# The landmarks' sums kept once: two products with the identity in place of a copy and a transpose

## The chip, the cores and the metric

The kernel runs on one core of one Trainium2 chip. A core has TensorE (PE, with its weight loads shown apart as PEld), VectorE (DVE), ScalarE (ACT), GpSimd (POOL) and SyncE (SP, which issues most of the transfers here). The metric is the device time of one execution in microseconds; the kernel before took 1337.75 us in the median of 3 runs (1334.39 to 1339.83).

## The reference

The program computes a Nystrom attention with 32 landmarks for 8 batches of 8 heads, 576 positions and 64 values per head, then a layer with a squared ReLU (512 to 2048 to 512), then a layer of 8 experts of which each token takes one. All is in float32. The change touches the landmarks alone: each is the mean of 18 neighbouring positions of q or of k, and every score of the attention has a landmark on one side.

```python
def _attn_ref(q, k, v):
    m = 32
    q_lm = q.reshape(B, H, m, S // m, D).mean(axis=3)
    k_lm = k.reshape(B, H, m, S // m, D).mean(axis=3)
    A = sm(q, k_lm)
    Bm = sm(q_lm, k_lm)
    C = sm(q_lm, k)
    Z = Bm.transpose(0, 1, 3, 2) / (norm1(Bm) * norminf(Bm) + 1e-06)
    for _ in range(6):
        Z = 2 * Z - Z @ Bm @ Z
    return A @ Z @ C @ v

def _moe_ref(x, w_in, w_out):
    r = np.maximum(x @ w_in, 0.0)
    return (r * r) @ w_out

# then, for each expert e and its tokens:
#   out[mask] = gate * eom * (np.maximum(x[mask] @ w1[e], 0) @ w2[e])
```

## The kernel before

One batch after the other passes through two kinds of work. The attention of a batch is a chain of small steps (`unit`), and the first layer of a batch is a stream of large matmuls (`gemm`). The attention of batch 0 stands alone at the start (`prologue`), beside the conversion of the weights `w_in` and `w_out` (`convert`, lines 146 to 167: ACT, DVE and POOL work on each piece). From then on the steps of later batches are woven between the matmuls of `gemm`: at each point of `gemm` a counter decides whether the next step of the attention is issued (`point`). The last stage are the experts (`experts`), with no attention in it.

In `gemm`, `hp` (line 998) is the hidden layer in six matmuls of 288 columns, ACT makes its ReLU (1009) and square `gh` (1014), DVE the rest `gl` of the square (1011, 1015), and `second` adds 12 matmuls into `acc` (1048). Nearly all matmuls of these streams are in fp32r with 128 x 128 weights.

A landmark step begins with the sums. q and k of a batch come in two groups of four heads (`hg`), 128 partitions (4 heads x 32 landmarks) by 18 positions by 64 values. `sums` adds the 18 positions on DVE in two halves of 32 values (line 382) and lets POOL copy the 64 sums beside themselves (line 385), so that a row has them twice. `landmarks` transposes these 128 columns on PE (line 349, with `self.ident`): the 64 values of a landmark then lie on partitions 0 to 63 and again on 64 to 127, four heads by 32 landmarks along the free axis. ACT copies both groups from the bank in PSUM to `lm` (line 447). The scores need both halves, since one half of the heads (or of the positions) is taken from partitions 0 to 63 and the other from 64 to 127. There are 8 batches x q and k x 2 groups = 32 sums, copies and transposes.

Names in the rows: `t` is a group of q or k as loaded, `sums` the sums, `bank` a bank of PSUM, `ident` the identity, `lm` the landmarks, `x` q or k with values on partitions, `eu`, `dg` and `bc` the iteration for the inverse, `wt` the small matrix Z C v of a batch, which is multiplied with `w` (a piece of `w_in`) in two matmuls into the two halves of a bank (line 872 loads `w`), `gb` and `ab` the split operands of `hp`. Attention matmuls are issued through `matmul` (line 346) and `transpose` (line 349), so rows are told apart by their tiles.

The order on each engine isn't the order of the code: the framework's scheduler deals the instructions out by priorities and its own reckoning of when each is ready. The attention of batch 0 has high priority (`URGENT`), and `follow` holds a few instructions behind others. On one engine the instructions run in the order dealt, so one that waits holds all behind it.

Of the kernel before, what the change touches and what calls it, by code (L numbers as in the profile page):

```python
# [9 lines left out]
F32 = mybir.dt.float32  # L10
# [4 lines left out]
ALU = mybir.AluOpType  # L15
AX = mybir.AxisListType
# [3 lines left out]
B, H, S, D = 8, 8, 576, 64  # L20
# [63 lines left out]
class Kernel:  # L84
# [290 lines left out]
    def sums(self, u, nm, hg):  # L375

        if hg == 0:
            u[nm + "s"] = self.sm.tile([128, 2, 2, D], F32, tag=f"{nm}s", name="sums", bufs=1)
        s, t = u[nm + "s"][:, hg], self.qk[nm, u["b"], hg]
        for d in range(0, D, D // 2):  # L380
            ds = slice(d, d + D // 2)
            self.nc.vector.tensor_reduce(  # L382
                out=s[:, 0, ds], in_=t[:, :, ds].rearrange("p s d -> p d s"), axis=AX.X, op=ALU.add
            )
        self.nc.gpsimd.tensor_copy(out=s[:, 1], in_=s[:, 0])

    def transposed(self, u, nm, hg, i):

# [50 lines left out]
    def landmarks(self, u, nm):  # L439
        nc = self.nc  # L440
        pd = self.bank()
        for hg in range(2):
            self.transpose(
                pd[:, 128 * hg:128 * hg + 128], u[nm + "s"][:, hg].rearrange("p c d -> p (c d)"), self.ident
            )
        lm = u[nm + "l"] = self.sm.tile([128, 2, 4, LM], F32, tag=f"{nm}l", name="lm", bufs=1)
        nc.scalar.copy(out=lm.rearrange("p g h l -> p (g h l)"), in_=pd[:, 0:256])

# [1049 lines left out]
```

## Time and profile before

| | |
|---|---|
| median of 3 runs | 1337.75 us (1334.39 to 1339.83) |
| profiled execution | 1340.34 us, span 1338.5 us |
| mean granted clock of TensorE | 0.977 |
| PE busy | 1275.7 us, 95% of the span |
| DVE busy | 781.5 us, 58% |
| ACT busy | 633.6 us, 47% |
| POOL busy | 384.5 us, 29% |
| sums on DVE (line 382) | 64 x 1165 ns, 71.2 us |

Busy time is the time in which an engine had an instruction at work; PE's matmuls are pipelined, so that starts follow each other more closely than their durations say. The shares are means over stages that are bound by different things, so the rows below are taken by stretch. In the chain of waits a piece such as "PE bank L349 x2" is what PE did from one start to the next piece's.

### The profile page before, as it was taken

The page shows a single profiled execution, that of the slowest core. Times are in us where ns is not written, and L with a number is a line of the kernel's source. Part 1 is how long each engine was busy: PE and PEld are TensorE (multiplying, and loading weights), DVE is VectorE, ACT ScalarE, POOL GpSimd, SP SyncE. Part 2 cuts the span into 40 slices and gives each one's busy share as a digit, 9 for nine tenths or more (in the row PEclk, how much of TensorE's full clock was granted, in tenths as well). Part 3 has the DMA queues.
Part 4 walks back from the last instruction along what each step waited for, and adds up shares of the span by engine and source line. Part 5 has one row for each costly group of instructions (what it writes and reads, how often), then busy time and mean ns, then how long its engine had stood idle before and what let it go on. Part 6 is the DMA issues. An engine that isn't in the chain of part 4 may idle for free.

```text
span 1338.5 us, 25101 instructions
## 1 busy us (share of the span) xinstructions
PE 1275.7 (95%) x9458; PEld 1114.2 (83%) x9458; DVE 781.5 (58%) x1743; ACT 633.6 (47%) x1402; POOL 384.5 (29%) x311
## 2 busy tenths in 40 slices
PE   6587999999999999999999999999999999999997
PEld 4276868688788888898989999998888888888886
DVE  7999868768769897687653433454423233233231
ACT  5596454445535557545654344344334334334331
POOL 3566112113013034313622112024323323233120
PEclk7588999999999999999999999999999999999999
DMA  9866283462623247613652112014344354342321
GB/s 324 273 222 192 86 269 85 173 199 89 217 70 112 72 127 211 172 63 95 206 146 67 43 35 67 1 48 146 99 130 139 100 156 120 109 150 92 116 93 38
DMA packets 126587, 172.38 MB, mean 129 GB/s; under 512 B 10558, under 2 KB 84062, under 8 KB 126462
## 3 DMA queue, kind: packets, MB, share of 16 engines
q1 hardware_dynamic: 126030, 170.11, 41.6%
q8 instruction: 76, 1.25, 0.4%
q0 software_dynamic: 288, 0.43, 0.1%
q14 instruction: 49, 0.40, 0.1%
q10 hardware_dynamic: 144, 0.20, 0.0%
HBM read 128.19 MB, written 42.51 MB: 128 GB/s over the span
## 4 chain that ended last, share of the span: by engine, by line
PE 74%; DVE 11%; DMA 7%; ACT 3%; issue 2%; POOL 1%; SPq 1%; POOLq 0%; DVEq 0%; ACTq 0%
PE acc L1048 24%; PE hp L1238 15%; PE y L1274 13%; PE hp L998 11%; PE bank L346 6%; PE y L1286 2%; DMA raw<-in_moe_w_in_dram 2%; DVE sums L382 2%; DVE gl L1015 2%; DMA g<-gs 2%; DVE g L1011 1%; PE pl L1075 1%; DVE m L164 1%; DMA w<-win 1%; DMA t<-in_q_dram 1%
## 5 line engine op out<-in xcount | busy, mean ns | idle before, releaser
L1048 PE MATMUL acc<-gh,wo 128*128 128x288 f32 x2048 | 459.2, 300 | 1.6 <-POOL wo L191 0.7
L1048 PEld LDWEIGHTS acc<-gh,wo 128*128 128x128 f32 x2048 | 344.1, 190 | 27.1 <-issue 18.2
L1048 PE MATMUL acc<-gl,wo 128*128 128x288 f32 x1024 | 290.3, 301 | 10.2 <-DVE gl L1015 9.7
L998 PE MATMUL hp<-ab,gb 128*128 128x288 f32 x1536 | 254.8, 301 | 0.9 <-ACT r L1009 0.5
L998 PEld LDWEIGHTS hp<-ab,gb 128*128 128x128 f32 x1536 | 217.7, 189 | 19.6 <-issue 6.9
L1011 DVE TENSOR_TENSOR g<-r 128x288 f32<-128x288 f32 x239 | 130.3, 546 | 162.5 <-ACT r L1009 161.7
L1009 ACT ACTIVATE r<-hp 128x288 f32<-128x288 f32 x256 | 105.8, 413 | 245.1 <-PE hp L998 240.6
L1238 PEld LDWEIGHTS hp<-xs,s 128*128 128x128 f32 x1536 | 210.7, 188 | 9.0 <-issue 0.9
L1238 PE MATMUL hp<-xs,s 128*128 128x288 f32 x1536 | 215.5, 295 | 0.0
L1048 PEld LDWEIGHTS acc<-gl,wo 128*128 128x128 f32 x1024 | 194.6, 190 | 22.8 <-DVE gl L1015 17.5
L1274 PE MATMUL y<-s,h 128*128 128x512 f32 x768 | 190.3, 395 | 0.0
L1274 PEld LDWEIGHTS y<-s,h 128*128 128x128 f32 x768 | 141.0, 188 | 29.4
L1015 DVE TENSOR_TENSOR gl<-g,gh 128x288 fp32r<-128x288 f32 x256 | 143.2, 560 | 26.8 <-ACT gh L1014 8.9
L191 POOL TENSOR_TENSOR s<-r,s 128x512 fp32r<-128x512 f32 x64 | 83.1, 1299 | 245.6 <-ACT s L188 245.6
L191 DVE TENSOR_TENSOR s<-r,s 128x512 fp32r<-128x512 f32 x64 | 53.1, 830 | 154.4 <-ACT s L188 154.4
L191 POOL TENSOR_TENSOR gb<-gr,gb 128x512 fp32r<-128x512 f32 x56 | 74.5, 1331 | 226.6 <-ACT gb L188 143.6
L188 ACT CAST s<-r 128x512 fp32r<-128x512 f32 x128 | 78.2, 616 | 118.8 <-PE y L1286 92.6
L1247 DVE SCALAR_TENSOR_TENSOR h<-hp,h 128x64 fp32r<-128x64 f32 (+2 forms) x192 | 62.6, 354 | 109.5 <-ACT h L1244 109.5
L1014 ACT ACTIVATE gh<-r 128x288 fp32r<-128x288 f32 x256 | 114.4, 447 | 6.4
L1244 ACT ACTIVATE h<-hp 128x288 fp32r<-128x288 f32 x128 | 52.6, 411 | 132.1 <-PE hp L1238 118.2
L382 DVE TENSOR_REDUCE sums<-t 128x32 f32<-128x576 f32 x64 | 71.2, 1165 | 9.3 <-DMA t<-in_q_dram 5.8
L191 POOL TENSOR_TENSOR xs<-xr,xs 128x1152 fp32r<-128x1152 f32 x16 | 45.7, 2860 | 68.3 <-ACT xs L188 63.2
(195 smaller groups left out, 1350.8 us busy)
## 6 DMA issues: line engine op xcount, KB each, us to landing
r<-in_moe_w_dram SPq DMA_DIRECT2D x128, 256.0 KB
w<-win SPq DMA_DIRECT2D x80, 256.0 KB
gr<-g SPq DMA_DIRECT2D x56, 256.0 KB
t<-in_k_dram SPq DMA_DIRECT2D x16, 576.0 KB
t<-in_q_dram SPq DMA_DIRECT2D x16, 576.0 KB
v<-in_v_dram SPq DMA_DIRECT2D x48, 192.0 KB
x_d<-x SPq DMA_DIRECT2D x16, 576.0 KB
xr<-x_d SPq DMA_DIRECT2D x16, 576.0 KB
```

The source lines that it names most:

```text
L188: hi = self.nc.scalar.copy(out=t[:, 0], in_=raw)
L191: (lo_eng or self.nc.gpsimd).tensor_tensor(out=t[:, 1], in0=raw, in1=t[:, 0].bitcast(F32), op=ALU.subtract)
L346: self.last_pe = self.nc.tensor.matmul(out, **kw)
L382: self.nc.vector.tensor_reduce(out=s[:, 0, ds], in_=t[:, :, ds].rearrange("p s d -> p d s"), axis=AX.X, op=ALU.add)
L998: mm = nc.tensor.matmul(hp[:, 0:HC], lhsT=g[:, l, hg, fs], rhs=at[:, r, hg, :], start=(i == 0), stop=(i == 5))
L1009: nc.scalar.activation(out=r, in_=hp[:, 0:HC], func=ACTF.Relu, scale=1.0 / 256)
L1011: nc.vector.tensor_tensor(out=g2, in0=r, in1=r, op=ALU.mult)
L1014: nc.scalar.activation(out=gh, in_=r, func=ACTF.Square)
L1015: nc.vector.tensor_tensor(out=gl, in0=g2, in1=gh.bitcast(F32), op=ALU.subtract)
L1048: nc.tensor.matmul(acc[m][:, 0:HC], lhsT=self.wo[f][:, l, ms], rhs=r, start=(f == 0 and i == 0), stop=(f == NFC - 1 and i == 2),)
L1238: nc.tensor.matmul(hp[:, 0:HC], lhsT=s1[:, l, kk, :], rhs=xs[j, c][:, r, kk, :], start=(k == 0), stop=(k == 3 * KD - 1),)
L1274: mm = nc.tensor.matmul(acc[t], lhsT=l, rhs=s2[:, r, :], start=(first and k == 0), stop=(last and k == 2))
```

## The change

`sums` keeps the 64 sums once (the tile has half the size), and the copy on POOL is gone. `landmarks` no longer transposes. For each group it makes two matmuls with the sums as weights (128 x 64) and the identity as moving operand (128 columns), one into partitions 0 to 63 and one into 64 to 127 of the same columns of the bank. That is four matmuls in f32 per landmark step in place of two transposes, 64 in all in place of 32; the profile shows such an f32 matmul as two rows. DVE's reductions and ACT's copy to `lm` are as they were.

```diff
     def sums(self, u, nm, hg):
         if hg == 0:
-            u[nm + "s"] = self.sm.tile([128, 2, 2, D], F32, tag=f"{nm}s", name="sums", bufs=1)
+            u[nm + "s"] = self.sm.tile([128, 2, D], F32, tag=f"{nm}s", name="sums", bufs=1)
         s, t = u[nm + "s"][:, hg], self.qk[nm, u["b"], hg]
         for d in range(0, D, D // 2):
             ds = slice(d, d + D // 2)
             self.nc.vector.tensor_reduce(
-                out=s[:, 0, ds], in_=t[:, :, ds].rearrange("p s d -> p d s"), axis=AX.X, op=ALU.add
+                out=s[:, ds], in_=t[:, :, ds].rearrange("p s d -> p d s"), axis=AX.X, op=ALU.add
             )
-        self.nc.gpsimd.tensor_copy(out=s[:, 1], in_=s[:, 0])
...
     def landmarks(self, u, nm):
         pd = self.bank()
         for hg in range(2):
-            self.transpose(
-                pd[:, 128 * hg:128 * hg + 128], u[nm + "s"][:, hg].rearrange("p c d -> p (c d)"), self.ident
-            )
+            for p in (slice(0, D), slice(D, 2 * D)):
+                self.matmul(
+                    pd[p, 128 * hg:128 * hg + 128], lhsT=u[nm + "s"][:, hg], rhs=self.ident, start=True, stop=True
+                )
```

The scheduler deals the changed program out anew. Lines behind `landmarks` are one higher in the new program (1048 is 1049, 998 is 999). On PE, the start of the program, batch 0 before (rows of one instruction or of several alike, with their number in the list):

```order
1 L349 MATMUL bank<-ident,t 128x128 x18
2 L349 MATMUL bank<-ident,sums 128x128 x4
3 L346 MATMUL bank<-x,lm 32x288 x7
4 L346 MATMUL bank<-lm 32x32 x8
5 L346 MATMUL bank<-x,lm 32x288 x9
```

and now:

```order
1 L349 MATMUL bank<-ident,t 128x128 x16
2 L346 MATMUL bank<-ident,sums 64x128
3 L349 MATMUL bank<-ident,t 128x128
4 L346 MATMUL bank<-ident,sums 64x128
5 L349 MATMUL bank<-ident,t 128x128
6 L346 MATMUL bank<-ident,sums 64x128 x6
7 L346 MATMUL bank<-x,lm 32x288 x7
8 L346 MATMUL bank<-lm 32x32 x8
9 L346 MATMUL bank<-x,lm 32x288 x9
```

The products of the first groups stand between the transposes of `t`, and the eight of batch 0 are issued one by one as their sums come.

On PE in batch 2, the landmarks of k between the matmuls of `gemm`, before:

```order
304 L1048 MATMUL acc<-gl,wo 128x288
305 L1048 MATMUL acc<-gh,wo 128x288
306 L349 MATMUL bank<-ident,sums 128x128 x2
307 L1048 MATMUL acc<-gl,wo 128x288
308 L1048 MATMUL acc<-gh,wo 128x288
309 L1048 MATMUL acc<-gl,wo 128x288
310 L1048 MATMUL acc<-gh,wo 128x288
311 L998 MATMUL hp<-ab,gb 128x288 x6
312 L1048 MATMUL acc<-gh,wo 128x288
```

and now:

```order
300 L1049 MATMUL acc<-gh,wo 128x288
301 L346 MATMUL bank<-ident,sums 64x128 x4
302 L1049 MATMUL acc<-gl,wo 128x288
303 L1049 MATMUL acc<-gh,wo 128x288
304 L1049 MATMUL acc<-gl,wo 128x288
305 L1049 MATMUL acc<-gh,wo 128x288
306 L999 MATMUL hp<-ab,gb 128x288 x6
307 L346 MATMUL bank<-w,wt_1890 64x512
308 L1049 MATMUL acc<-gh,wo 128x288
```

Four matmuls stand where two transposes stood, and around them the matmuls of `wt` with `w` have moved against those of `gemm`.

On POOL, the first rows behind the constants, before:

```order
11 L385 COPY sums<-sums 128x64 x4
12 L167 TENSOR_TENSOR wf<-m,r 128x512 x7
13 L385 COPY sums<-sums 128x64
14 L167 TENSOR_TENSOR wf<-m,r 128x512
15 L477 TENSOR_TENSOR aa<-aa,ma 128x576
16 L167 TENSOR_TENSOR wf<-m,r 128x512 x2
17 L477 TENSOR_TENSOR aa<-aa,ma 128x576
```

and now:

```order
11 L167 TENSOR_TENSOR wf<-m,r 128x512 x8
12 L478 TENSOR_TENSOR aa<-aa,ma 128x576
13 L167 TENSOR_TENSOR wf<-m,r 128x512 x2
14 L478 TENSOR_TENSOR aa<-aa,ma 128x576
15 L167 TENSOR_TENSOR wf<-m,r 128x512 x2
16 L191 TENSOR_TENSOR ab<-at,ab 128x576
```

The copies of the sums are gone and nothing else has moved here; the conversion's additions (`wf`) follow each other directly.

## Rows read from the trace of the kernel before

**Rows 1.** stretches: us, busy us of PE PEld DVE ACT POOL, clock, DMA

```profile
0.00:80.00 80.00, 51.82 (x445) 30.34 (x446) 70.56 (x152) 50.63 (x115) 35.58 (x39) 0.74 0.92 298
80.00:130.00 50.00, 40.13 (x367) 35.58 (x366) 48.28 (x76) 39.10 (x93) 34.84 (x26) 0.86 0.59 181
130.00:700.00 570.00, 555.74 (x4655) 478.15 (x4656) 434.42 (x985) 302.41 (x701) 156.18 (x140) 1.00 0.47 142
```

**Rows 2.** the chain of waits from 130 to 700 us, its shares by line

```profile
by line: PE acc L1048 32.3%; PE hp L998 15.7%; PE bank L346 13.2%; DMA g<-gs 3.6%; issue 3.5%; DVE sums L382 3.4%; DVE gl L1015 2.8%; DVE g L1011 2.5%; DMA w<-win 2.0%; DVE x L413 1.6%; DMA v<-in_v_dram 1.5%; PE bank L349 1.5%; PE pl L1075 
```

**Rows 3.** the tile of the sums: ns min/median/max, starts

```profile
L382 DVE TENSOR_REDUCE sums<-t x64: 1111/1169/1225, 4.7 to 595.7; 128x32 f32<-128x576 f32 x64
L385 POOL COPY sums<-sums x32: 230/266/563, 7.0 to 596.9; 128x64 f32<-128x64 f32 x32
...
L349 PE MATMUL bank<-ident,sums x32: 270/272/477, 8.7 to 597.9; 128*128 128x128 f32 x32
...
  PE bank L349: 5.2, 5
```

**Rows 4.** waits of PE, 130 to 700 us: us, times, longest

```profile
PE acc L1048 <- DVE gl L1015: 4.4, 7, 1.1
...
PE bank L349 <- POOL sums L385: 1.4, 2, 0.9
```

**Rows 5.** timeline at 420 us around one transpose: start, us

```profile
420.42 0.24 POOL L385 COPY sums<-sums 128x64 f32<-128x64 f32 x1 [3.38 <-DVE sums L382]
...
420.71 0.44 PE L349 MATMUL bank<-ident,sums 128*128 128x128 f32 x2 [0.43 <-POOL sums L385]
```

**Rows 6.** timeline to 15 us, the last copy and transpose of batch 0

```profile
13.23 0.36 POOL L385 COPY sums<-sums 128x64 f32<-128x64 f32 x1 [1.86 <-DVE sums L382]
...
13.65 0.48 PE L349 MATMUL bank<-ident,sums 128*128 128x128 f32 x1 [1.89 <-POOL sums L385]
```

**Rows 7.** chain of waits, 162 to 169 us: start, us, what

```profile
162.07 1.87 PE bank L346 x8
163.94 0.99 PE hp L998 x6
...
165.46 1.01 PE bank L346 x4
166.47 0.73 PE acc L1048 x4
167.20 0.22 PE bank L349 x2
167.42 0.54 PE acc L1048 x4
167.96 0.80 PE hp L998 x6
```

**Rows 8.** the lines of f32 matmuls on line 346, by operands and shape

```profile
L346 PE MATMUL bank<-x,lm x512: 402/427/686, 14.6 to 638.2; 64*32 64x288 f32 x171
...
L346 PE MATMUL bank<-eu,dg x168: 217/275/350, 130.1 to 649.2; 128*128 128x96 f32 x140, 128*128 128x64 f32 x28
...
L346 PE MATMUL bank<-w,wt x96: 592/592/644, 162.0 to 361.7; 128*64 128x512 f32 x96
```

**Rows 9.** the chain of waits from 148 to 154 us

```profile
151.93 0.42 PE bank L346 x4
152.34 0.82 PE hp L998 x6
```

**Rows 10.** timeline, DVE's subtractions beside POOL's work

```profile
415.58 1.45 POOL L191 TENSOR_TENSOR gb<-gr,gb 128x512 fp32r<-128x512 f32 x1 [0.91 <-ACT gb L188]
...
415.81 1.54 DVE L1015 TENSOR_TENSOR gl<-g,gh 128x288 fp32r<-128x288 f32 x1
...
427.34 0.44 DVE L1015 TENSOR_TENSOR gl<-g,gh 128x288 fp32r<-128x288 f32 x1
427.48 0.40 POOL L385 COPY sums<-sums 128x64 f32<-128x64 f32 x1 [3.35 <-DVE sums L382]
```

## The prediction

> **What bounds the kernel now.** I read the busy time of the engines by stretch first, then the chain of waits, then everything that touches the tile of the sums, and last the PE timeline beside matmuls of the new shape.
>
> The stretches [rows 1] show three regimes. Up to 80 us DVE works 70.56 of 80 us and the DMA share is 0.92, while PE works 51.82 us. From 80 to 130 us DVE works 48.28 of 50 us, so it is the bound, and PE has 10 us to spare. From 130 to 700 us PE works 555.74 of 570 us, so only 14.3 us are free. The last transpose of sums starts at 597.9 us [rows 3], so nothing that the change touches lies behind 700 us. The chain of the third stretch [rows 2] says the same less sharply: its three largest entries are PE's lines, 61% together, and DVE's sums have 3.4%. So in the third stretch a microsecond added to PE costs close to a microsecond, and one taken from POOL, 156.18 us busy of 570, is worth nothing unless PE or DVE waited for it.
>
> The sums [rows 3]: 64 reductions on DVE, 32 copies on POOL of 266 ns, 32 transposes on PE. PE stood idle before a transpose, waiting for a copy, 5.2 us in five waits [rows 3]. Only two of these, 1.4 us, are in the third stretch [rows 4], where 24 of the 32 transposes lie (those of batches 2 to 7); the other three belong to batch 0, 13.65 us being the last.
>
> **The change part by part.** *The copies go.* 32 copies of 0.27 us are 8.6 us of POOL's 384.51. POOL isn't the bound in any stretch, and PE's two late waits don't vanish whole. At 420.42 us the copy itself starts only when DVE's reduction has ended, and PE starts 0.29 us later [rows 5]. The hop of 0.29 us goes, the reduction stays, and DVE's sums are what is late next. Two waits: 0.6 us. What stood behind the copies on POOL, the subtractions for gb and aa, may start earlier; with POOL busy 156.18 of 570 us [rows 1] I price that at nothing.
>
> *In the prologue* the last copy starts at 13.23 us and PE at 13.65 [rows 6], so 0.42 us are saved. Against the median of 0.272 [rows 3] this transpose took 0.48 us, in a stretch whose mean granted clock is 0.74 [rows 1], so partly at the lower level (1.2 GHz); four rows of products in its place take longer by what I estimate below from wt, 0.215 us a pair at 2.4 GHz and twice that at 1.2, and so give back most of the 0.42. The order on DVE, which does 70.56 of these 80 us, is unchanged up to batch 1. I take zero, and half a microsecond either way for the range.
>
> *The transposes become products.* Each landmark had two transposes. The chain shows such a pair as one piece of 0.22 us, followed by four acc matmuls in 0.54 us [rows 7], 0.135 each, their usual pace. Now it has four f32 products with 64 columns of weights and 128 moving columns, two for the lower and two for the upper half of the partitions. No row of before has just this. The nearest is wt, 128 x 64 weights into the two halves of a bank, in f32 too, with 512 moving columns. One pair takes 1.01 us and two pairs together take 1.87 [rows 7]: a second pair adds 0.86, so a train has about 0.15 us of its own and 0.86 per pair at 512 columns, or 0.215 at 128 if it goes with the columns. (That it does go with the columns is borne out by the medians of a row in [rows 8], 592 at 512, 427 at 288, 275 at 96.) What stands behind such a train is late too: acc x4 takes 0.73 us instead of 0.54, hp x6 0.99 instead of 0.80 [rows 7], so 0.20 us each time.
>
> The Trainium skill, "TensorEngine Tiling (Array Packing)", Key Properties, says that changing the tiling mode drains TensorE; by that rule the 0.20 us is the drain, and the trace agrees that there is one. The same page's Restrictions say that column tiling excludes transpose mode for f32, so the halves could not be had as two cheap transposes; no run here shows that.
>
> A landmark's train is then 0.15 + 2 x 0.215 = 0.58, with the 0.20 behind it 0.78, against 0.22 before. In the new order batches 2 to 7 have 24 pairs in 14 trains, two of which stand beside a wt train of the same shape, so that 12 pay the fixed 0.35 us: 24 x 0.215 + 12 x 0.35 - 24 x 0.11 = 5.2 + 4.2 - 2.6 = 6.7 us. The bounds come from the rows on both sides. Low: a train of two f32 matmuls at 96 columns without halves takes 0.42 with hardly a late start behind it (hp 0.82) [rows 9], so +0.2 per landmark, 2.4 us for 12. High: 288 columns in place of 128, 0.15 + 2 x 0.48 + 0.20 - 0.22 = 1.1 per landmark, 13 us. I take 6.7, since 128 lies near 96.
>
> Batch 1 has its eight products in one train between 80 and 130 us: 4 x 0.215 + 0.35 - 0.44 = 0.8 us, covered by PE's 10 us of slack beside DVE. If that cover were gone, 0.8 us would be added.
>
> *What hides the 6.7 us* is only PE's own idle time of 14.3 us. Where PE would have waited anyway, a train costs nothing. I leave 85% standing: 5.7 us. Less the two hops this is +5.1 us.
>
> *The order.* The program's instructions are dealt out anew by a scheduler, and from batch 2 on acc, hp and attention steps stand in other places on PE, DVE, ACT and SP. The work is the same. I price the deal at 0 in the sum and keep it as a rival.
>
> **The sum.** The profiled execution took 1340.34 us with a span of 1338.5; +5.1 gives 1345.4. Its median in three runs is 1337.75, 2.6 lower, so the same change gives 1342.9; I say 1342.5. That is +0.36%. About 0.5% (6.7 us) is what a measurement of this kernel can tell from no change, so this counts as no change, not far from the edge of slower at 1344.4.
>
> **The rivals.** *A, the order loses (slower).* In the third stretch PE waits for DVE's gl in seven places with 4.4 us [rows 4]. If in the new order the reductions of 1.17 us stand more often ahead of gl on DVE, and PE's idle 14.3 us grow by half, 7 us are added: 1350. It decides as soon as 2 us more are lost than I reckoned. For it: DVE is busy in 76% of the stretch, 434.42 of 570 us [rows 1], so PE has little lead on it. Against it: before has the same mixture, and the deal can win as well.
>
> *B, the halves don't overlap (slower).* Then a pair takes 0.43 us, 24 x 0.215 = 5.2 us more: 1348. Against it speaks wt, two of whose pairs in 1.87 us would take about twice that if they ran one behind the other.
>
> *C, PE's idle time swallows the price (same).* 14.3 us would be room for 6.7. Then only the hops remain: 1337. Against it: the trains stand between acc and hp, where PE works through, and only two of the 24 late transposes had PE waiting for a copy.
>
> *D, DVE is relieved (faster).* On DVE an elementwise operation with two SBUF inputs suffers beside POOL: gl took 1.54 us beside POOL's subtraction at 415.81, but 0.44 beside the copy at 427.48 [rows 10]. If each copy had held DVE for its own time, 8.6 us would come back, all of it where DVE bounds or feeds PE. With the five waits of 5.2 us gone whole and the low price of 2.4 us this gives 1337.75 - 8.6 - 5.2 + 2.4 = 1326. Against it is the row at 427.48: there the copy was the longer one, 0.40 instead of 0.24, and gl was not. The Trainium skill, "GPSIMD Engine Reference", Specifications, says that GpSimd shares its SBUF interfaces with VectorE, with contention for DVE instructions with two SBUF inputs; by that rule alone D would be likely, and the trace agrees for POOL's subtraction, not for its copy.
>
> **How the numbers follow.** Forecast 0.50 (own range 1338 to 1347; three tenths of it beyond 1344.4), A 0.18, B 0.06, C 0.12, D 0.14. Slower: 0.15 + 0.18 + 0.06 = 0.39. Same: 0.35 + 0.12 = 0.47. Faster: 0.14. The range reaches down past C into the upper part of D, since a deal that wins also ends there, and up past A: 1331 to 1352.
>
> **What would show it.** On PE the sums' group has 64-column weights and mean rows near 0.3 us; a landmark's piece in the chain is near 0.58 us instead of 0.22, and hp or acc behind it are 0.20 longer. POOL has 32 instructions fewer and PE no wait for POOL's sums. PE's idle time from 130 to 700 us stays near 14 us while the stretch grows by about 5. It is wrong if the stretch after 130 us is shorter than before (D or a lucky deal), if a piece lasts 0.9 us or more (B), if the idle time falls by as much as the products add (C), or if PE's waits for gl grow by several microseconds (A). A change before 130 us of more than 1 us would also be outside this account.

## The result and the profile after

The changed kernel took 1345.23 us (median of 6 runs, 1342.84 to 1347.08) beside 1337.83 us (1334.39 to 1339.83) of the kernel before: ratio 1.0052, 95% interval 1.0036 to 1.0068, so 7.0 us slower, between 4.8 and 9.1. A second series of runs gave 1.0055 [1.0036, 1.0074]. The forecast was 1342.5, the range 1331 to 1352. The number lies inside; what follows shows that half of the reasons behind it did not hold.

The stretches of the changed kernel, in the columns of [rows 1]:

```profile
0.00:80.00 80.00, 52.32 (x456) 30.88 (x457) 71.13 (x152) 50.87 (x115) 33.63 (x32) 0.72 0.91 299
80.00:130.00 50.00, 37.92 (x383) 31.70 (x382) 48.11 (x79) 38.49 (x91) 34.05 (x25) 0.94 0.61 193
130.00:700.00 570.00, 558.37 (x4678) 476.59 (x4678) 434.54 (x978) 300.31 (x697) 148.37 (x117) 1.00 0.46 141
```

From 130 to 700 us PE works 558.37 us where it worked 555.74, so its idle time is 11.6 us instead of 14.3, and the work that used to end in this stretch now ends about 6 us later. DVE is as busy as it was, POOL 7.8 us less.

The tile of the sums in the changed kernel, which answers to [rows 3] (ns min/median/max, starts; below, PE's waits that an instruction on this tile ended: us, times):

```profile
L346 PE MATMUL bank<-ident,sums x128: 272/273/476, 8.3 to 600.0; 128*64 128x128 f32 x128
L382 DVE TENSOR_REDUCE sums<-t x64: 1107/1171/1220, 4.7 to 598.6; 128x32 f32<-128x576 f32 x64
...
  PE bank L346: 3.5, 5
```

64 products leave 128 rows. POOL's copies are gone. A reduction on DVE takes 1171 ns at the median, where it took 1169.

PE's waits from 130 to 700 us in the changed kernel, which answer to [rows 4]:

```profile
PE acc L1049 <- DVE gl L1016: 5.9, 12, 1.1
...
PE bank L346 <- DVE sums L382: 0.8, 3, 0.4
```

POOL is no longer waited for. DVE's gl is waited for in 12 places, against 7.

A piece of the chain of waits of the changed kernel around one landmark, the same place as [rows 7] (start, us, what):

```profile
165.59 1.01 PE bank L346 x4
166.60 0.73 PE acc L1049 x4
167.32 0.59 PE bank L346 x8
167.91 0.72 PE acc L1049 x4
```

The train of four products is the piece of eight rows with 0.59 us, where two transposes took 0.22. The four acc matmuls behind it take 0.72 instead of 0.54.

Last, two rows of ACT's timeline in the kernel before: activations that take a half batch out of `acc`, as milestones (start, us):

```profile
141.12 0.69 ACT L1054 ACTIVATE x<-acc 128x288 f32<-128x288 f32 x2
...
319.98 0.41 ACT L1054 ACTIVATE x<-acc 128x288 f32<-128x288 f32 x1 [0.32 <-PE acc L1048]
```

The same two in the changed kernel:

```profile
146.39 0.70 ACT L1055 ACTIVATE x<-acc 128x288 f32<-128x288 f32 x2
...
319.83 0.41 ACT L1055 ACTIVATE x<-acc 128x288 f32<-128x288 f32 x1 [0.31 <-PE acc L1049]
```

At 141 us the changed kernel is 5.3 us behind, at 320 us it is level again. A price that adds up landmark by landmark does not look like that, although one milestone of one trace is a weak sign. So two theories went to the chip. *Price*: the products themselves cost the time. *Order*: the new deal of instructions on the engines costs it.

### The profile page after: what moved, and what is told of

The parts are those of the page before. It is cut to its first block, busy times and chain, and to the rows that moved or that the text cites. A ratio compares the mean times of both kernels' runs of the same rounds, so it can differ in the third digit from the quotient of the medians.

```text
span 1344.7 us, 25243 instructions
## 1 busy us (share of the span) xinstructions
PE 1282.9 (95%) x9554; PEld 1115.8 (83%) x9554; DVE 783.1 (58%) x1743; ACT 633.4 (47%) x1402; POOL 374.0 (28%) x279
## 4 chain that ended last, share of the span: by engine, by line
PE 76%; DVE 10%; DMA 5%; ACT 3%; issue 3%; POOL 1%; SPq 0%; POOLq 0%; DVEq 0%; ACTq 0%
PE acc L1049 25%; PE hp L1239 15%; PE y L1275 13%; PE hp L999 12%; PE bank L346 7%; PE y L1287 2%; DVE sums L382 2%; DMA g<-gs 2%; PE pl L1076 1%; DVE m L164 1%; DVE gl L1016 1%; DVE g L1012 1%; DVE m L163 1%; DMA gr<-g 1%; DMA t<-in_q_dram 1%
## 5 line engine op out<-in xcount | busy, mean ns | idle before, releaser
L382 DVE TENSOR_REDUCE sums<-t 128x32 f32<-128x576 f32 x64 | 71.2, 1166 | 11.1 <-DMA t<-in_q_dram 8.5
```

What stands on the lines that cost most here:

```text
L382: self.nc.vector.tensor_reduce(out=s[:, ds], in_=t[:, :, ds].rearrange("p s d -> p d s"), axis=AX.X, op=ALU.add)
```

## The experiments

Both kernels leave their order to the scheduler. To part work from order, most of the kernels below carry a recorder. It lists each engine's instructions as the program issues them and, at the end, holds them to a table with dependencies that need no semaphore:

```diff
+        for e, t in _ORDER.items():
...
+            for k in order:
...
+                for i in made[k]:
+                    if last is not None:
+                        self.follow(i, last)
+                    last = i
```

The table is the order of the kernel before, or of the changed one, or one spliced from both. In the traces of these kernels every row has the recorder's line, `pin.txt:10`, so rows are told apart by tiles. Leaving out the rows of the sums and the landmarks, the traces of e1, e3, e4 and e7 show the order of before row by row on PE, DVE, ACT and POOL, and those of e2 and e11 that of the changed kernel. The changed order has no place for POOL's copies, so in e2 and e11 the scheduler places them. No run holds the work of before to its own order from end to end; the nearest is e5, which bounds what the recorder itself costs (0.3 us, between -1.3 and 2.0).

| kernel | work | order | us | ratio to before, 95% interval | difference, us |
|---|---|---|---|---|---|
| changed | products | changed | 1345.2 | 1.0052 [1.0036, 1.0068] | +7.0 |
| e1 | products | before | 1340.0 | 1.0026 [1.0015, 1.0037] | +3.5 |
| e2 | transposes | changed | 1343.8 | 1.0055 [1.0035, 1.0075] | +7.4 |
| e3 | products twice | before | 1343.3 | 1.0047 [1.0028, 1.0065] | +6.3 |
| e4 | products, copies kept | before | 1341.1 | 1.0036 [1.0021, 1.0052] | +4.8 |
| e5 | transposes | changed, then before | 1337.9 | 1.0002 [0.9990, 1.0015] | +0.3 |
| e6 | transposes | before, then changed | 1344.4 | 1.0050 [1.0034, 1.0066] | +6.7 |
| e7 | full-width products | before | 1339.5 | 1.0017 [1.0005, 1.0029] | +2.3 |
| e8 | one transpose | before | 1334.1 | 0.9976 [0.9961, 0.9992] | -3.2 |
| e9 | transposes | spliced | 1369.9 | 1.0259 [1.0233, 1.0286] | +34.6 |
| e10 | products (changed again) | changed | 1345.1 | 1.0055 [1.0036, 1.0074] | +7.4 |
| e11 | transposes (e2 again) | changed | 1343.8 | 1.0056 [1.0037, 1.0075] | +7.5 |
| e12 | one transpose | its own deal | 1340.2 | 1.0025 [1.0012, 1.0038] | +3.3 |

The differences are the ratio less one, times the 1337 us of before.

**e1 and e2: work and order apart.** e1 has the changed work, in the order of before (a pair of products stands where a transpose stood). e2 has the work of before in the changed order.

> The changed work (four column-split products per landmark step, no copies on GpSimd) with every engine's instructions held to the order of the kernel before; a pair of products stands where a transpose stood. Price theory (the time is in the products themselves: 0.59 us for a piece of two trains' rows where 0.22 stood, and 0.2 us on the train behind): the same 6 to 7 us as the changed kernel, 1343.5 to 1345.5 us, ratio to before 1.0045 to 1.0055. Order theory (the time comes from the new deal of work between half batches, which has lost 5.3 us by 141 us in the trace of after): about 1338 us, ratio 0.998 to 1.002. A mixture of both lands between, near 1341.

> The work of before (two transposes per landmark step, copies on GpSimd) with TensorE, VectorE, ScalarE and the DMA queue held to the order of the changed kernel. Price theory: as before, 1338 us +- 2, ratio 0.9985 to 1.0015. Order theory: the changed kernel's 1345 us, ratio 1.005. If the order gains and the products lose, this kernel would be faster than before: 1335.

e1 costs 3.5 us, between 2.0 and 4.9: half of what price foretold, and not nothing. e2 costs 7.4 us, between 4.7 and 10.0, without a single product: as much as the whole change. So the changed order alone is enough for the result, and price alone isn't. The two don't add up: 3.5 + 7.4 is 10.9, and the change costs 7.0 to 7.4, a gap only just clear of the noise.

Pieces of the chain of e1 around a landmark:

```profile
163.73 0.59 PE bank pin.txt:10 x8
164.31 0.73 PE acc pin.txt:10 x4
```

The train and the late start behind it are as in the changed kernel. PE's waits from 130 to 700 us in e1 (us, times, longest):

```profile
PE acc pin.txt:10 <- DVE gl pin.txt:10: 3.4, 5, 1.1
...
PE bank pin.txt:10 <- DVE sums pin.txt:10: 0.4, 2, 0.3
```

The same waits in e2:

```profile
PE acc pin.txt:10 <- DVE gl pin.txt:10: 5.9, 11, 1.2
PE bank pin.txt:10 <- POOL sums pin.txt:10: 3.0, 4, 1.0
```

In the order of before, gl is waited for in 5 places with the products (e1) and in 7 without [rows 4]; the other kernels held to that order have 4 to 8 (e3, e4, e7, e8). In the changed order it is 12 places with them and 11 without (e2). The number of places goes with the order. And in the changed order PE waits 3.0 us for POOL's copies, against 1.4 [rows 4].

**e3 and e4: more of the suspected cost, and the copies back.** Both follow e1. e3 issues each pair twice:

```diff
-            for p in (slice(0, D), slice(D, 2 * D)):
+            for p in (slice(0, D), slice(D, 2 * D)) * 2:
```

e4 keeps the tile of twice the size and the copy:

```diff
+        self.nc.gpsimd.tensor_copy(out=s[:, 1], in_=s[:, 0])
```

> As the first, with each pair of products issued twice (the second pair writes the same values over the first): 28 pairs more after 130 us. Price theory, with the pair at the 0.215 us of the forecast (the halves of the columns run side by side): the train grows from 0.59 to 1.0 us, 28 x 0.215 = 6.0 us over the first kernel, near 1350. If the two halves ran one after the other, a pair would cost 0.43 us and the step 12 us, near 1356. If TensorE has idle time there that swallows it (the third rival of the prediction): no step, as the first within 1.5 us.

> As the first, with GpSimd's 32 copies of the sums kept, read by nobody. Price theory: the copies were hidden, so the same as the first within 1 us. The theory that VectorE is relieved by the missing copies (the fourth rival): up to 32 x 0.27 = 8.6 us slower than the first; a VectorE reduction beside a copy would then be longer than 1.17 us in this trace.

The chain of e3 around a landmark:

```profile
165.45 1.02 PE bank pin.txt:10 x16
166.47 0.73 PE acc pin.txt:10 x4
```

The second two pairs add 1.02 - 0.59 = 0.43 us to the train, 0.215 a pair, as forecast; the halves do overlap, and the late start does not grow. In the order of before 24 pairs stand behind 130 us, in 13 trains (the expectation reckoned with 28), so that is 24 x 0.215 = 5.2 us on PE's path. The time grew by 2.8 us from e1 to e3 (the intervals allow about 0 to 5.5): about half of it by the medians, possibly all of it, and not 12.

e4 stands 1.3 us above e1, with intervals that overlap widely. DVE's reductions in e4, beside the copies on POOL:

```profile
pin.txt:10 DVE TENSOR_REDUCE sums<-t x64: 1102/1166/1206, 4.8 to 596.8; 128x32 f32<-128x576 f32 x64
pin.txt:10 POOL COPY sums<-sums x32: 236/300/763, 7.1 to 598.0; 128x64 f32<-128x64 f32 x32
```

1166 ns with the copies, 1171 ns without them in the changed kernel: no relief. A kernel that keeps the copies is not 8.6 us slower than one without; up to some 4 us the intervals don't exclude.

**e5 and e6: where the order costs.** Work of before; e5 takes the changed order first and that of before afterwards, e6 the reverse. The splice was set at about 300 us (for PE it fell near 350), in a stretch in which the two orders don't differ: e6 shows the same rows as before until 422 us on PE, 431 on DVE and 422 on ACT.

> The work of before (two transposes per landmark step, GpSimd's copies). Every engine keeps the order of the changed kernel for what it starts in the first 300 us, and the order of before for the rest; at that point both orders have done the same set of instructions on every engine. The order alone cost 7.2 us with before's work over the whole program. If it loses in the fill, where the changed order is behind by some 5 us at 141 us: 1342 to 1344 us here, ratio 1.004 to 1.006. If what is lost there is regained by 320 us, as the traces of both changed-order kernels suggest: 1336 to 1338 us, ratio 0.999 to 1.001.

> The counterpart: before's work, the order of before for the first 300 us on every engine, the order of the changed kernel for the rest. If the order loses between 335 and 714 us (batches 3 to 7, where the changed-order traces fall behind by 3 to 6 us): 1339 to 1344 us, ratio 1.002 to 1.005. If it loses in the fill: about 1337 us, ratio 0.999 to 1.001. Whatever comes, the two halves should add up to the 7.2 us if the order's cost is a sum over places.

e5 costs 0.3 us (at most 2.0), e6 6.7. So the lag of 5.3 us at 141 us costs nothing that shows in the end; the milestone also scatters, 137.7 us in e1 and 141.4 in e6, both in the order of before up to there. The price of the order arises behind 422 us. PE's waits from 422 to 710 us in e5, which has the order of before there:

```profile
PE acc pin.txt:10 <- DVE gl pin.txt:10: 1.4, 2, 0.9
PE bank pin.txt:10 <- POOL sums pin.txt:10: 1.4, 2, 0.9
```

The same in e6:

```profile
PE acc pin.txt:10 <- DVE gl pin.txt:10: 3.6, 7, 1.1
PE bank pin.txt:10 <- POOL sums pin.txt:10: 3.0, 4, 1.0
PE bank pin.txt:10 <- ACT wi pin.txt:10: 1.3, 1, 1.3
PE acc pin.txt:10 <- ACT gh pin.txt:10: 1.0, 1, 1.0
```

The first two waits add 2.2 and 1.6 us in e6; wi (0.7 in e5) and gh add 1.6 more. With the small waits that are not shown, PE waits 9.9 us in e6 and 5.3 in e5, 4.6 us more. The two profiled executions lie 8.4 us apart (1349.11, the slowest of e6, and 1340.69), so waits are about half of it.

The other half is busy time. The stretch below runs between two matmuls, the same two in every kernel; in between PE has the same matmuls everywhere, only the landmarks' own differ (us; idle is the length less PE's busy time):

| kernel | work | order there | from, to | length | PE busy | idle |
|---|---|---|---|---|---|---|
| before | transposes | before | 393.22, 726.81 | 333.59 | 325.07 | 8.5 |
| e5 | transposes | before | 396.68, 727.27 | 330.59 | 324.04 | 6.6 |
| e2 | transposes | changed | 393.41, 729.78 | 336.37 | 326.72 | 9.7 |
| e11 | transposes | changed | 390.51, 729.55 | 339.04 | 328.07 | 11.0 |
| e6 | transposes | changed from 422 | 394.80, 735.47 | 340.67 | 329.47 | 11.2 |
| e1 | products | before | 392.41, 724.00 | 331.59 | 326.83 | 4.8 |
| changed | products | changed | 393.99, 733.11 | 339.12 | 330.61 | 8.5 |
| e10 | products | changed | 394.01, 734.20 | 340.19 | 331.77 | 8.4 |

Traces of one order and one work differ by 3 to 4 us here. At the means, the transposes take 332.1 us in the order of before and 338.7 in the changed one: 6.6 us more, 3.1 of them idle and 3.5 busy, on the same matmuls. In the changed kernel PE is idle no longer than in the kernel before, 8.5 us in both; its extra 5.5 us are all busy time. Why the same matmuls keep PE busy longer in the changed order is not shown. A granted clock of 0.99 instead of 1.00 in this stretch goes with it in e6, e10 and e11, but not in e2 and the changed kernel.

How a wait for gl comes about is seen near 490 us. DVE's timeline in the changed kernel (start, us):

```profile
489.98 0.46 DVE L1012 TENSOR_TENSOR g<-r 128x288 f32<-128x288 f32 x1 [1.51 <-ACT r L1010]
490.36 4.44 DVE L382 TENSOR_REDUCE sums<-t 128x32 f32<-128x576 f32 x4
494.71 0.45 DVE L1016 TENSOR_TENSOR gl<-g,gh 128x288 fp32r<-128x288 f32 x1
```

The matmul on PE that waited for this gl:

```profile
495.21 0.40 PE L1049 MATMUL acc<-gl,wo 128*128 128x288 f32 x1 [0.86 <-DVE gl L1016]
```

DVE's timeline in e1, with the same work in the order of before:

```profile
488.45 0.46 DVE pin.txt:10 TENSOR_TENSOR g<-r 128x288 f32<-128x288 f32 x1 [0.54 <-ACT r pin.txt:10]
489.02 0.46 DVE pin.txt:10 TENSOR_TENSOR gl<-g,gh 128x288 fp32r<-128x288 f32 x1
489.81 4.50 DVE pin.txt:10 TENSOR_REDUCE sums<-t 128x32 f32<-128x576 f32 x4 [0.34 <-PE bank pin.txt:10]
```

In the changed deal the four reductions, 4.44 us, stand between a g and its gl; in that of before they stand behind gl. PE waited 0.86 us for that gl. This one wait is the mechanism of rival A at work.

**e7: passes or column split.** Before's order and copies; each transpose becomes one product over the full width:

```diff
-            self.transpose(
-                pd[:, 128 * hg:128 * hg + 128], u[nm + "s"][:, hg].rearrange("p c d -> p (c d)"), self.ident
+            self.matmul(
+                pd[:, 128 * hg:128 * hg + 128], lhsT=u[nm + "s"][:, hg].rearrange("p c d -> p (c d)"),
+                rhs=self.ident, start=True, stop=True,
             )
```

> Before's order and GpSimd's copies; each of the 32 transposes becomes a product of the same 128x128 shape with the identity, without the split into halves of the columns. It has the two passes of a float32 product and no change of the tiling. If the price of the changed work is in the passes: a train of 4 rows takes about 0.43 us where 0.22 stood, and with the exposure of about a half that the first and third kernels show the time is +1.5 us over before, 1338 us. If the price is in the column split (the train behind starting 0.2 us late): within 0.5 us of before.

The chain of e7 around a landmark:

```profile
165.33 0.44 PE bank pin.txt:10 x4
165.77 0.53 PE acc pin.txt:10 x4
```

Two products have four rows and take 0.44 us, twice the two transposes; nothing behind them is late. 24 x 0.11 = 2.6 us of work cost 2.3 us [0.7, 3.9]. So passes cost, and the split adds to them: e1 stands 1.2 us above e7, and spares besides the copies' hop. That the split costs extra is shown by the chain (0.59 and 0.73 against 0.44 and 0.53), by the times alone it isn't: the intervals overlap.

**e8: fewer rows on PE.** The sums of both groups lie side by side, one transpose takes them, and ACT writes the landmarks into both halves of the partitions:

```diff
-        for hg in range(2):
...
+        self.transpose(pd[:, 0:128], u[nm + "s"].rearrange("p g d -> p (g d)"), self.ident)
-        nc.scalar.copy(out=lm.rearrange("p g h l -> p (g h l)"), in_=pd[:, 0:256])
+        for p in (slice(0, D), slice(D, 2 * D)):
+            for hg in range(2):
+                nc.scalar.copy(out=lm[p, hg].rearrange("p h l -> p (h l)"), in_=pd[D * hg:D * hg + D, 0:128])
```

> Before's order without GpSimd's copies; the sums of both groups of heads lie side by side, and one 128x128 transpose per landmark step takes them both to TensorE's bank, where two transposes stood. ScalarE writes the landmarks into both halves of the partitions with four copies of 64x128 in place of one of 128x256. If TensorE's time is what counts: 14 x 0.11 = 1.5 us less after 130 us, -0.8 us at an exposure of a half, 1336 us. If the landmarks' way to the scores counts (four copies, some 0.9 us more than the 0.37 us of the one): up to 14 x 0.9 us slower where the products behind wait for them, and ScalarE is 10 us busier over the span.

1334.1 us, 3.2 us less than before, between 1.1 and 5.2: the one version that is faster than before. The chain of e8 around a landmark:

```profile
170.97 0.11 PE bank pin.txt:10
171.08 0.27 PE acc pin.txt:10 x2
```

ACT's copies in e8 (ns min/median/max, starts):

```profile
pin.txt:10 ACT COPY lm<-bank x64: 242/260/265, 9.6 to 592.7; 64x128 f32<-64x128 f32 x64
```

PE's piece is 0.11 us. Four copies of 0.26 us took the place of one of 0.37, and no wait for them shows in the time. It gained more than the 0.8 us expected. Twelve transposes fewer behind 130 us (the expectation reckoned with 14) are 1.3 us, and PE's wait for the sums fell from 1.4 us [rows 4] to 0.9, so 0.5 more. Together 1.8 us, inside the interval; whether anything more was gained, the runs don't say.

**e9: a splice that missed.** Meant to put the change of order at 490 us. The place was counted in rows of the trace, of which an f32 product leaves two, so on PE it fell at 628 us, while the other engines changed over near 490 as meant.

> Before's work; every engine in the order of before for what it starts in the first 490 us, in the order of the changed kernel for the rest. The changed order from 300 us on cost 6.7 us. If it is lost in the last batches' fillers (in its trace TensorE's lag grows from 530 us on, where it waits for VectorE's gl and for the landmarks' sums): the same 5 to 7 us here, ratio 1.004 to 1.0055. If it is lost between 300 and 490 us: 1337 us, ratio 0.999 to 1.001. Spread evenly: about 3.5 us.

It answers nothing of its question; within the part behind 422 us the cost of the order was not placed more closely. But it shows what an order is worth. For 140 us PE ran in one order and its feeders in another, with the same work, and that cost 34.6 us. PE's waits from 486 to 630 us in e9:

```profile
PE acc pin.txt:10 <- DVE gl pin.txt:10: 11.6, 5, 3.5
PE hp pin.txt:10 <- ACT r pin.txt:10: 4.6, 6, 1.4
```

**e10 and e11: what the products cost in the changed order.** The changed kernel and e2 once more, both on one chip.

> The changed kernel once more, beside the next kernel on the same chip: 1344 us, ratio 1.0036 to 1.0068. Together they tell what the products cost in the changed order. If prices add up (order 7.2 us, products 3.5 us): 3.5 us above the next kernel. If the changed order hides the products and their saved hop (its TensorE waits 3.0 us for GpSimd's copies of the sums, against 1.4 us in the order of before): within 1.5 us of the next.

> Before's work in the changed order once more, on the chip of the run before: 1344 us, ratio 1.0035 to 1.0075.

Between the two stand 1.3 us by the medians and nothing by the ratios, 1.0055 and 1.0056; the first pair of ratios, 1.0052 and 1.0055, says the same. In the changed order the products cost 0, give or take some 2.5 us. One reason is in the waits: there PE waits 3.0 us for POOL's copies (e2) and 0.8 for DVE's sums when the copies are gone, so the change gives back 2.2 us, against 1.0 in the order of before (1.4 [rows 4] to 0.4 in e1). Whether this is all, the noise of 2.5 us does not let one say.

**e12: the better version in its own deal.** The edit of e8 without the recorder.

> One 128x128 transpose per landmark step and four copies on ScalarE, as in the eighth kernel, but with the order that the kernel's own dealing then makes instead of the order of before. If the dealt order is what a change like this hangs on: anything from 1331 to 1343 us, so that the gain of 3 us may be gone; if the order has no price of its own: 1334 us, ratio 0.996 to 0.999.

3.3 us slower than before, between 1.6 and 5.1. The same work in the order of before is 3.2 faster. So the new deal again costs some 6.5 us, on an edit that takes work away from PE and POOL and adds copies on ACT alone. How it costs them is not known: of the 4.5 us between the traces of e8 and e12, 3.5 lie before the first of the two matmuls of the table under e6 (388.39 against 391.92 us), so not where the changed kernel lost.

## Why the prediction came out as it did

*The number held by luck, through two errors of opposite sign.* The forecast was +5.1 us from the products less the hops, and 0 from the order. Measured are +3.5 for the work in the order of before, and, in the order that the changed kernel got, +7.4 for that order and about 0 for the work on top. By the prediction's own line of 0.5% (1344.4 us) the outcome is "slower", to which it gave 0.39, and not "same", its likeliest at 0.47.

*The train* was right to two hundredths: 0.59 us against 0.58 worked out from wt, 0.72 behind it against 0.74. A further pair costs 0.215, as taken (e3). B, halves one behind the other, is out. The 0.20 us late start shows only behind the products that split the columns (e1, e3) and not behind full-width ones (e7); so far the trace agrees with the drain that the Trainium skill, "TensorEngine Tiling (Array Packing)", Key Properties, states for a change of the tiling mode.

*The hops* were taken at 0.6 us and are 1.0 in the order of before, 2.2 in the changed one.

*"I leave 85% standing"* is not refuted. e1 shows 3.5 + 1.0 = 4.5 of 6.7 us, two thirds, with an interval from 45% to 88%. e3's second pairs show 2.8 of 5.2, e7 2.3 of 2.6, both with intervals that hold 85%. Where the added rows fill time in which PE would have waited, the later waits shrink: gl 4.4 us in seven places before, 3.4 in five in e1. C, that idle time swallows all of it, is out in the order of before (2.0 us at least remain); in the changed order e10 and e11 don't exclude it.

*"I price the deal at 0"* is the step that failed. The order alone costs 7.4 us (e2, and again e11), behind 422 us as far as the times can tell (e5, e6). Rival A named a mechanism that is there, reductions ahead of gl on DVE: the waits of gl grew from 4.4 us in seven places to 5.9 in eleven (e2), and the waits for the copies from 1.4 to 3.0. But these are 3.1 of the 7.4 us. A let PE's idle time grow by 7 us; the table under e6 gives 3.1 of 6.6 to idle time, and in the changed kernel PE's idle time did not grow. That A's 7 us and the order's 7.4 agree is luck in part, and the cause of the other half stays open. I held against it that the deal can win as well. Two changed programs were dealt out freely here and both deals lost, by 7.4 and 6.5 us.

*"PE's idle time stays near 14 us"* failed with it: it is 11.6 in the fixed stretch. *"A change before 130 us of more than 1 us would be outside this account"*: the lag of 5.3 us at 141 us, just behind that line, costs nothing that shows (e5). A lag at one milestone of a program whose order has changed need not be a loss.

*D* at its 8.6 us is out by e4, and by DVE's 1171 ns; a relief of a few microseconds is not excluded.

## What to carry to other kernels

Where a scheduler deals out the instructions, an edit buys a new order with it, and on a path as full as this one (PE busy 97% from 130 to 700 us) the order can weigh more than the edit; part the two by holding the new work to the old order, and the old work to the new one. A gain of 3 us was there for the one-transpose version and was lost in its deal. Prices from neighbouring rows were good to two hundredths of a microsecond per train; how much of them shows in the time stayed uncertain by a third or more. And a wait that is found in the trace need not be the whole price: set it beside the total before calling it the cause.

## What the runs showed of the hardware

An f32 product of 128x128 with the identity takes twice the time of the transpose of the same shape (0.44 against 0.22 us for two, e7), and split into two halves of the columns the four rows' worth becomes 0.59 us with 0.2 us more on the train behind. ACT copies 64 partitions into the other half of the partitions in 0.26 us (e8), no more than straight (all 64 copies lie between 242 and 265 ns).
